# Loads of q and k move behind the threshold rows in SyncE's queue, with other ranks in the planner

## The chip, the core and the metric

The kernel runs on one core of one Trainium2 chip. The metric is device time in microseconds (us) of one execution; lower is better. Five instruction streams run side by side: TensorE (PE: matmuls), VectorE (DVE), ScalarE (ACT), GpSimd (POOL) and SyncE (SP, which here only issues DMA transfers). Each of them works through its own instructions strictly in the order in which they stand in the program, and waits at the head of its queue when data are missing.

## The reference

The input has 8 batches of 8 heads, 576 positions, 64 values per head, in float32. A thresholded attention feeds a feed-forward block:

```python
scores = scale * np.matmul(q, k.transpose(0, 1, 3, 2))
thresh = np.max(scores, axis=-1, keepdims=True) - tau
scores = np.where(scores >= thresh, scores, -1000000000.0)
scores = scores - np.max(scores, axis=-1, keepdims=True)
attn = np.exp(scores)
attn = attn / (np.sum(attn, axis=-1, keepdims=True) + 1e-09)
o = np.matmul(attn, v)                     # 64 heads
x = o.transpose(0, 2, 1, 3).reshape(4608, 512)
h = x @ w_in                               # 512 x 2048
g = h * (1.0 / (1.0 + np.exp(-1.702 * h)))
out = g @ w_out                            # 2048 x 512
```

The two weight matrices arrive in float64 (`wide` in the kernel): the kernel loads their bits and turns them into float32 itself.

## The kernel before

**Attention** works on 32 pairs of heads, numbered n from 0; four pairs make a batch, and "the fifth pair" is pair 4. One pair goes through these tasks (names of functions, lines of the profile):

- `load_qk(n, 0)` and `load_qk(n, 1)` (L246): q and k of the pair, four DMAs each, issued by SP (for pair 0, k by ACT). `load_v` (L256, L260): four DMAs on SP.
- `prep` (L358): DVE transposes q, then k, in blocks. This frees the raw buffer for the pair after next.
- `scores` (L382, tail L375): PE, four tiles of keys and a tail; `keep` (L405): ACT copies them to SBUF.
- `in_groups` (L419), `over_tiles`, `over_groups` (L425 to L438): DVE finds the maximum of each column. For pairs 0 to 7, `lower_rows` (L454, L459) subtracts tau and leaves a small tile `flat`; `row_out` (L471) sends it to DRAM as the threshold row, and `row_in` (L480, L482) fetches it back broadcast over all partitions, as `mb` and `mbt`. All three DMA steps are in SP's queue. From pair 8 on, `lower` and `spread_max` do this on DVE alone.
- `sub` (L489, L491): DVE subtracts the thresholds; `mask` (L500) and `exps` (L504): ACT.
- `values` and `sums_by_pe` (L518): PE multiplies by v, and for pairs 0 to 4 sums the weights; `one_row`, `spread_sums` (L547 to L568) and `place_x` (L585) on DVE put the normalized result into `xT`.

**The weights** come in 32 pieces of 128 x 512 values: 0 to 15 of `w_in`, 16 to 31 of `w_out`. `load_w` (L310, L311): POOL issues two DMAs of 512 KB for each into one of a few staging slots. `cv_ex` (L321), `cv_frac` (L335, L339) on DVE, `cv_power` (L329) on ACT and `cv_end` (L347) on DVE convert a piece, and `cv_end` frees its slot: pieces 6, 7, 8 and 9 wait for the slots of 0, 1, 2 and 3.

**The feed-forward block** starts when pairs 0 to 3 are placed: `first_blocks` does tokens 0 to 511 by plain matmuls, `mm1_0` (L640), `tanh` (L609), `gelu_0` (L646) and `mm2` (L622); `mm1_0(j)` needs the four converted pieces of its columns, and `mm2(i, p)` pieces 16+2p and 17+2p. After that, blocks of 256 tokens run with `mm1` (L600) and seven `product`s (L690) in Strassen's manner, while pairs 8 to 31 are threaded in between.

**The order on each engine** is not written out. A planner (`run_in_order`) plays the whole task graph through with fixed costs, and whenever an engine of this model is free it gives it the ready task of lowest rank. The rank is the pair's number plus an offset for the function's name (`EARLY` for pairs 0 to 7, `LATER` beyond, `CV` for conversions; weights have `W_IN`, `W_OUT`). The order of calls fixes the program's order. Costs, ranks and `after=` of a task act through this order alone: on the chip an instruction waits for the data and buffers that it uses and for those ahead of it on its engine.

```python
lq = task("SP", 2.0, r - 2.0, load_qk, n, 0, q0, take=own(n, "raw0"), lag=2.0)
lk = task("SP", 2.0 if n else 0.1, r - 2.0, load_qk, n, 1, q1, take=own(n, "raw1"), lag=2.0)
```

With `r = n`, loads of pair n rank two pairs ahead of its work, and start as soon as the raw buffers are free.

Of the kernel before, what the change touches and what calls it, by code (L numbers as in the profile page):

```python
# [30 lines left out]
def kernel(  # L31
# [37 lines left out]
    NPAIR = H // 2  # L69
# [59 lines left out]
    for x in ("raw0", "raw1", "qkT0", "qkT1", "mb"):  # L129
# [13 lines left out]
        "over_groups": -1.9,  # L143
        "sub": -0.29,
        "one_group": 0.95,
        "scores": -0.68,
        "spread_sums": 0.92,
        "sums_by_pe": 1.09,
        "in_groups": 0.61,
        "keep": -1.15,  # L150
    }
    LATER = {
        "in_groups": 0.38,
        "mask": -0.74,
    }
    CV = {
        "cv_power": 0.15,
    }

    def task(engine, cost, rank, f, *a, after=(), take=(), give=(), lag=0.06):  # L160
        if 0 <= rank < LAST:
            rank += CV.get(f.__name__, 0.0) + (EARLY if a[0] < 2 * NPAIR else LATER).get(f.__name__, 0.0)
        tasks.append((engine, cost, rank, f, a, [x for x in after if x is not None],
                      take, give, lag))
        return len(tasks) - 1
# [67 lines left out]
    def own(n, *pools):  # L233
        return tuple(x + "_apart" for x in pools) if n in APART else pools
# [527 lines left out]

    FFU = 1.722

    W_IN, W_OUT = (3.21, 1.53), (3.16, 2.2)
    ready_w, w_loads = [], []
    for i in range(len(pieces)):
        if i < n_in:
# [11 lines left out]
        m = task("ACT", 0.79, rank, cv_power, i, after=[e])  # L780
# [6 lines left out]
    tau_done = task("DVE", 1.0, -2.0, tau_terms, after=[warm])  # L787


    placed, ffn = {}, []  # L790
    last_mm2, t_ready = {}, []

    def first_blocks():
# [88 lines left out]
    for n in range(NP):  # L882
        gate = per_pair * (n - LEAD)
        after = ffn[gate : gate + 1] if gate >= 0 else []
        r = float(n)

        slow = 1.2 if n < NPAIR else 1.0
        q0, q1 = (nc.sync, nc.scalar) if n == 0 else (nc.sync, nc.sync)
        lq = task("SP", 2.0, r - 2.0, load_qk, n, 0, q0, take=own(n, "raw0"), lag=2.0)
        lk = task("SP", 2.0 if n else 0.1, r - 2.0, load_qk, n, 1, q1, take=own(n, "raw1"), lag=2.0)  # L890
        v_tail = f"v_t{n % 2}"
        lv = task("SP", 2.1, r - 1.2, load_v, n, take=("v_m", v_tail), lag=2.0)
        pq = task("DVE", 0.77, r, prep, n, 0, after=[lq], take=own(n, "qkT0"), give=own(n, "raw0"))
# [8 lines left out]
        for t in range(NKT + 1):  # L902
            tail = t == NKT
            copies = []
            if tail or n >= WHOLE:
# [5 lines left out]
                    take=("psA", "s_t") if tail else ("psA", "psA") + own(n, "s_m"),  # L911
                    give=own(n, "qkT0", "qkT1") + ("kd",) if tail else (),
                )
                after = [a]
                copies = [task("ACT", 0.65, r, keep, n, t, c, after=[a], give=("psA",)) for c in cs]
            else:
                for c in range(2):
# [3 lines left out]
                        take=("psA",) + (own(n, "s_m") if c == 0 else ()),  # L921
                    )
                    after = [a]
# [4 lines left out]
        if n < BY_DMA:  # L928
            a = task("DVE", 0.5, r, lower_rows, n, after=[a, tau_done], take=("row",))
            a = task("SP", 0.35, r, row_out, n, after=[a], lag=2.8)  # L930
            m = task(
                "SP", 1.5, r, row_in, n, after=[a], take=own(n, "mb") + ("mbt",), give=("row",),
                lag=5.0,
            )
        else:
            a = task("DVE", 0.7, r, lower, n, after=[a, tau_done])
            m = task("DVE", 1.38, r, spread_max, n, after=[a], take=own(n, "mb"))
        ws, subs = [], [m]
        for t in range(NKT + 1):
            tail = t == NKT  # L940
# [9 lines left out]
        if n < NPAIR:  # L950

            pv = den = None
            for t in every:
# [3 lines left out]
                    take=("psM", "psM") if first else (),  # L957
# [3 lines left out]
                    take=("psA",) if first else (), give=(back[t],) if t < NKT else ("s_t", "v_m", v_tail),  # L961
# [60 lines left out]
```

## Time and profile before

| | |
|---|---|
| six runs | median 1401.43 us, 1399.86 to 1404.77 |
| the profiled execution | 1402.07 us |
| its span in the profile | 1400.3 us (1.8 us lie around it) |
| PE busy | 1341.4 us, 96% of the span |
| DVE busy | 1037.6 us, 74% |
| ACT busy | 625.7 us, 45% |
| POOL busy | 281.9 us, 20% |
| granted TensorE clock, mean | 0.986 |

A row of the timeline tells start, length, engine, line, operation, tiles and count, and in brackets how long the engine was idle before it and what ended the wait. "SPq" and "POOLq" are the DMA-issuing queues. One fp32 matmul of the program appears as two records on PE.

### The profile page before, as it was taken

How to read it: one execution, taken by the hardware profiler on the slowest of the kernel's cores; microseconds unless marked ns; L12 is line 12 of the kernel's file. 1: busy time of each engine (PE TensorE's matmuls, PEld its weight loads, DVE VectorE, ACT ScalarE, POOL GpSimd, SP SyncE). 2: the span in 40 equal slices, each digit the busy share in tenths (PEclk: the TensorE clock that was granted, in tenths of full speed). 3: DMA queues.
4: the chain of work that ended last, by engine and by line, in shares of the span. 5: the costliest groups of instructions: out<-in, count | busy, mean ns of one | idle time of the engine just before them, and what ended most of it. 6: DMA issues, size and time to landing. Idle time of an engine off the chain costs nothing.

```text
span 1400.3 us, 18089 instructions
## 1 busy us (share of the span) xinstructions
PE 1341.4 (96%) x6856; PEld 1013.4 (72%) x6856; DVE 1037.6 (74%) x1773; ACT 625.7 (45%) x806; POOL 281.9 (20%) x374
## 2 busy tenths in 40 slices
PE   5648999999999999999999999999999999999998
PEld 3325774467777777777777777777777778888887
DVE  7859899898888888878988888888888886111111
ACT  5657454654444544455454455553545453100100
POOL 1201223123020122112120312020212212211211
PEclk9869999999999999999999999999999999999999
DMA  8656863311111111111111111101111100000000
GB/s 180 197 184 191 268 239 89 86 29 24 41 25 41 26 37 30 26 37 22 41 26 41 26 33 26 41 17 41 26 42 26 26 8 8 9 15 15 1 15 15
DMA packets 205727, 79.59 MB, mean 57 GB/s; under 512 B 192840, under 2 KB 192840, under 8 KB 205640
## 3 DMA queue, kind: packets, MB, share of 16 engines
q1 hardware_dynamic: 196072, 44.60, 14.9%
q0 software_dynamic: 7200, 33.55, 6.9%
q8 instruction: 54, 0.88, 0.2%
q10 hardware_dynamic: 2368, 0.30, 0.2%
q14 instruction: 33, 0.27, 0.1%
HBM read 68.93 MB, written 9.47 MB: 56 GB/s over the span
## 4 chain that ended last, share of the span: by engine, by line
PE 86%; DVE 7%; DMA 3%; issue 2%; SPq 1%; ACT 1%; POOL 0%; DVEq 0%; POOLq 0%; ACTq 0%
PE hps L600 32%; PE ops L690 28%; PE pv L518 10%; PE ps L382 9%; PE ops L622 3%; PE ps L375 2%; DVE s_m L489 1%; PE hps L640 1%; DVE part L419 1%; DVE arena L489 1%; SPq L246 1%; DMA w_out<-in_moe_w_in_dram 1%; DMA arena<-in_moe_w_out_dram 1%; DMA w_out<-in_moe_w_out_dram 1%; DVE qkT L358 0%
## 5 line engine op out<-in xcount | busy, mean ns | idle before, releaser
L600 PE MATMUL hps<-xT,w_in 128*128 128x256 f32 x2048 | 457.3, 381 | 0.0
L600 PEld LDWEIGHTS hps<-xT,w_in 128*128 128x128 f32 x2048 | 385.8, 190 | 67.3 <-issue 11.2
L419 DVE TRANSPOSE_TENSOR_REDUCE part<-s_m 128x36 f32<-128x1152 f32 x228 | 304.9, 1356 | 61.3 <-ACT s_m L405 57.9
L405 ACT COPY s_m<-ps 128x576 f32<-128x576 f32 x240 | 141.2, 642 | 243.3 <-PE ps L382 239.9
L690 PE MATMUL ops<-w_out,arena 128*128 128x256 f32 x1024 | 232.8, 381 | 0.0
L690 PEld LDWEIGHTS ops<-w_out,arena 128*128 128x128 f32 x1024 | 192.8, 190 | 33.6 <-issue 6.2
L609 ACT ACTIVATE th<-hps 128x512 f32<-128x512 f32 x144 | 85.4, 593 | 294.2 <-PE hps L600 280.7
L668 POOL TENSOR_TENSOR arena<-arena 128x256 f32<-128x256 f32 x64 | 58.6, 916 | 676.9 <-DVE arena L612 676.9
L500 ACT ACTIVATE s_m<-s_m 128x1152 f32<-128x1152 f32 x120 | 136.2, 1156 | 130.0 <-DVE s_m L489 129.2
L690 PE MATMUL ops<-arena 128*128 128x256 f32 x768 | 174.3, 381 | 0.0
L489 DVE TENSOR_TENSOR s_m<-s_m,mb 128x1152 f32<-128x1152 f32 x120 | 161.0, 1376 | 15.2 <-DMA mb<-row 14.5
L612 DVE SCALAR_TENSOR_TENSOR arena<-th,hps 128x512 f32<-128x512 f32 x128 | 87.2, 681 | 111.3 <-ACT th L609 109.3
L690 PEld LDWEIGHTS ops<-arena 128*128 128x128 f32 x768 | 144.8, 190 | 24.7 <-issue 4.6
L382 PE MATMUL ps<-qkT 64*128 64x288 f32 x960 | 150.1, 436 | 10.7 <-DVE qkT L358 9.4
L504 ACT ACTIVATE s_m<-s_m,shift,scl 128x1152 f32<-128x1152 f32 x120 | 157.3, 1342 | 0.9
L382 PEld LDWEIGHTS ps<-qkT 64*128 64x128 f32 x960 | 84.6, 191 | 69.0 <-issue 32.2
L518 PE MATMUL pv<-s_m,v_m 128*64 128x288 f32 x960 | 122.9, 409 | 0.0
L712 DVE SCALAR_TENSOR_TENSOR osb<-ops,osb 128x256 f32<-128x256 f32 x112 | 44.6, 410 | 99.5 <-PE ops L690 98.5
L518 PEld LDWEIGHTS pv<-s_m,v_m 128*64 128x64 f32 x960 | 66.5, 137 | 52.1 <-issue 8.8
L622 PE MATMUL ops<-w_out,arena 128*128 128x512 f32 x128 | 59.4, 613 | 2.8 <-DVE w_out L347 2.8
L640 PE MATMUL hps<-xT,w_in 128*128 128x256 f32 x256 | 58.0, 383 | 2.8 <-DVE arena L646 1.7
L670 POOL TENSOR_TENSOR arena<-arena 128x256 f32<-128x256 f32 x64 | 60.2, 941 | 0.0
(97 smaller groups left out, 1050.6 us busy)
## 6 DMA issues: line engine op xcount, KB each, us to landing
out_dram<-osb SPq DMA_DIRECT2D x36, 256.0 KB, 2.0
q_raw<-in_q_dram SPq DMA_DIRECT2D x120, 72.0 KB, 2.2
k_raw<-in_k_dram SPq DMA_DIRECT2D x116, 72.0 KB, 2.2
v_m<-in_v_dram SPq DMA_DIRECT2D x64, 128.0 KB, 2.3
w_out<-in_moe_w_in_dram POOLq DMA_DIRECT2D x12, 512.0 KB, 9.0
arena<-in_moe_w_out_dram POOLq DMA_DIRECT2D x12, 512.0 KB, 5.9
w_out<-in_moe_w_in_dram POOLq DMA_DIRECT2D x12, 511.6 KB, 9.9
arena<-in_moe_w_out_dram POOLq DMA_DIRECT2D x12, 511.6 KB, 7.0
```

Source lines behind the costliest of these rows:

```text
L382: nc.tensor.matmul(ps[:, h, 0:SH], lhsT=kT[ts(h, D), ts(t, P)], rhs=qT[ts(h, D), ts(c, SH)], start=True, stop=True,)
L405: nc.scalar.copy(out=o, in_=pss.pop((n, t, c))[:, :, 0:SH])
L419: nc.vector.tensor_reduce(out=o, in_=i, axis=AXL.X, op=op, apply_transpose=True)
L489: nc.vector.tensor_tensor(out=s, in0=s, in1=mb, op=ALU.subtract)
L500: nc.scalar.activation(out=s, in_=s, func=AF.Prelu, alpha=STEEP)
L504: nc.scalar.activation(out=s, in_=s, func=AF.Exp, scale=scl, bias=shift)
L518: nc.tensor.matmul(o[c][ts(h, D), 0:SH], lhsT=lhsT, rhs=rhs, start=(t == 0), stop=(t == NKT),)
L600: nc.tensor.matmul(hidden[j][:, ts(f, BLK)], lhsT=w_in[:, c, ds((f * HF + j) * P, P)], rhs=xTs[blk][:, c, :], start=(c == 0), stop=(c == N ...
L609: nc.scalar.activation(out=ths[j], in_=hidden[j], func=AF.Tanh, scale=GELU_SCALE / 2)
L612: nc.vector.scalar_tensor_tensor(out=g[:, :, j, :], in0=two(ths.pop(j)), scalar=1.0, in1=two(hidden.pop(j)), op0=ALU.add, op1=ALU.mult,)
L622: nc.tensor.matmul(acc[i], lhsT=g0[:, j, ts(i, P)], rhs=w_out[:, j, :], start=(j == 0), stop=(j == NFC - 1),)
L690: nc.tensor.matmul(banks[k][:, ts(o, HM)], lhsT=left[:, j, :], rhs=right[:, j, :], start=(j == 0), stop=(j == HF - 1),)
```

## The change

Three things are edited. Loads of q and k from pair 4 on get a dependency: they come after `spread[n - 2]`, which is `row_in` for pairs up to 7 and `spread_max` beyond. The planner's cost of such a load goes from 2.0 to 3.5 for pairs 4 to 7. And eight offsets and the rank of the first weight load are changed or added.

```diff
-        "scores": -0.68,
-        "spread_sums": 0.92,
-        "sums_by_pe": 1.09,
-        "in_groups": 0.61,
+        "scores": -1.85,
+        "spread_sums": 0.09,
+        "sums_by_pe": 1.93,
+        "in_groups": 1.37,
         "keep": -1.15,
+        "over_tiles": 0.88,
     }
     LATER = {
         "in_groups": 0.38,
         "mask": -0.74,
+        "prep": 0.98,
     }
     CV = {
         "cv_power": 0.15,
+        "cv_end": -0.38,
     }
...
-    W_IN, W_OUT = (3.21, 1.53), (3.16, 2.2)
+    W_IN, W_OUT = (3.92, 1.53), (3.16, 2.2)
...
+        behind = [spread[n - 2]] if n >= NPAIR else []
+        cost = 3.5 if NPAIR <= n < 2 * NPAIR else 2.0
+        lq = task("SP", cost, r - 2.0, load_qk, n, 0, q0, after=behind, take=own(n, "raw0"), lag=2.0)
+        lk = task(
+            "SP", cost if n else 0.1, r - 2.0, load_qk, n, 1, q1, after=behind,
+            take=own(n, "raw1"), lag=2.0,
+        )
...
+        spread[n] = m
```

No instruction is added or taken away; every engine gets the same instructions in another order. SP's queue from the first threshold row on (q4 is `load_qk(4, 0)`, row 2 is `row_out(2)` and `row_in(2)`, v2 is `load_v(2)`):

```
before: row 0, q4 k4, row 1, v2, q5 k5, row 2, v3, row 3, v4, q6 k6, v5, row 4, q7 k7, v6, row 5
after:  row 0, row 1, v2, row 2, q4 k4, v3, row 3, q5 k5, v4, v5, row 4, q6 k6, v6, row 5, q7 k7
```

DVE's queue, with "cv" for the conversion of a piece, "max" for `in_groups` and "fold" for `over_tiles`, `over_groups` and `lower_rows`, which end with the row's `flat` tile:

```
before: ... fold 1, prep 3, max 2, sub 1 (0-2), one_row 0, sub 1 (3-4), place 0 among cv 0 to 2 without
        their ends, prep 4, max 2 tail, fold 2, ends of cv 0 to 2, one_row 1, cv 3, most of cv 4,
        sub 2, place 1, end of cv 4, max 3, fold 3, ex and frac of cv 5 to 8 (ex 9), end of cv 5,
        sub 3 with one_row 2 in it, place 2, prep 5, cv 9 to 14 with one_row 3 in them,
        max 4 (0-1), place 3, ...
after:  ... prep 3, max 1 tail, fold 1, max 2, cv 0, cv 1, sub 1 with place 0 in it, max 2 tail, fold 2,
        cv 2 and 3, max 3 (0) among them, most of cv 4, sub 2 with one_row 1 in it, place 1, prep 4,
        end of cv 4, max 3 (1-4), fold 3, cv 5 to 7, ex 8, sub 3 with place 2 in it, prep 5,
        rest of 8, cv 9 to 13, ex 14, one_row 3, place 3, rest of 14, cv 15, max 4, ...
```

On PE, `sums_by_pe` and `values` of pairs 0 to 3 stand tile by tile in turn, where before all sums of a pair came first; the first blocks follow behind pair 3 as before. POOL's order is nearly unchanged: the copies `prep_kd` of pairs 4, 5 and 6 stand at other places among the weight loads.

More of the change, by code (lines that the diff above doesn't have):

```diff
@@ L787 @@
     tau_done = task("DVE", 1.0, -2.0, tau_terms, after=[warm])
-    placed, ffn = {}, []
+    placed, spread, ffn = {}, {}, []
     last_mm2, t_ready = {}, []
@@ L888 @@
         q0, q1 = (nc.sync, nc.scalar) if n == 0 else (nc.sync, nc.sync)
-        lq = task("SP", 2.0, r - 2.0, load_qk, n, 0, q0, take=own(n, "raw0"), lag=2.0)
-        lk = task("SP", 2.0 if n else 0.1, r - 2.0, load_qk, n, 1, q1, take=own(n, "raw1"), lag=2.0)
+        behind = [spread[n - 2]] if n >= NPAIR else []
[5 more added lines that the diff above has]
+        )
         v_tail = f"v_t{n % 2}"
```

## Prediction

> **What bounds the kernel now.** First the page's slices: where is PE not full?
>
> ```profile
> PE   5648999999999999999999999999999999999998
> ...
> DVE  7859899898888888878988888888888886111111
> ...
> PEclk9869999999999999999999999999999999999999
> DMA  8656863311111111111111111101111100000000
> ```
>
> A slice is 35 us. Only the first four show idle PE; there DVE is the fuller engine and DMA is busy. In windows, PE is busy for 175.9 us up to 230 us (54 us idle), and for all but about 5 us of the rest. So a gain can come only from the start, and a loss can come anywhere. Next, SP's timeline in that stretch, to see what the rows wait for:
>
> ```profile
> 26.68 14.13 SPq L246 DMA_DIRECT2D k_raw<-in_k_dram  x4
> 40.90 0.37 SPq L471 DMA_DIRECT2D row<-flat  x1
> ...
> 60.04 4.01 SPq L246 DMA_DIRECT2D q_raw<-in_q_dram  x4
> 64.17 14.36 SPq L246 DMA_DIRECT2D k_raw<-in_k_dram  x4
> 78.63 0.59 SPq L471 DMA_DIRECT2D row<-flat  x1
> 81.36 0.36 SPq L480 DMA_DIRECT2D mb<-row  x1
> ...
> 146.65 9.74 SPq L246 DMA_DIRECT2D q_raw<-in_q_dram  x4
> 156.43 10.25 SPq L246 DMA_DIRECT2D k_raw<-in_k_dram  x4
> ```
>
> Then DVE's timeline: when is a row ready, when is it back, when are the four pairs placed?
>
> ```profile
> 46.38 3.90 DVE L489 TENSOR_TENSOR arena<-arena 128x1152 f32<-128x1152 f32 x3 [4.08 <-DMA arena<-row]
> ...
> 63.17 0.23 DVE L459 STREAM_TRANSPOSE flat<-flat 32x64 f32<-32x64 f32 x1
> ...
> 85.38 5.16 DVE L489 TENSOR_TENSOR s_m<-s_m,mb 128x1152 f32<-128x1152 f32 x4 [14.50 <-DMA mb<-row]
> ...
> 100.25 0.23 DVE L459 STREAM_TRANSPOSE flat<-flat 32x64 f32<-32x64 f32 x1
> ...
> 136.26 0.91 DVE L585 TENSOR_TENSOR xT<-pv,rc 128x256 f32<-128x256 f32 x4
> ```
>
> Row 2 is ready at 63.4 and leaves at 78.63, behind q5 and k5, which SP needs 18.5 us to issue while weights stream (POOL issued pieces 3 to 9 from 53.8 to 70.8). DVE stands for 14.50 us. Row 1, ready at 35.9, leaves at 40.90 behind k4: 4.08 us. Last PE's timeline:
>
> ```profile
> 136.70 19.91 PE L640 MATMUL hps<-xT,w_in 128*128 128x256 f32 x90 [1.06 <-DVE xT L585]
> ...
> 225.93 4.34 PE L622 MATMUL ops<-w_out,arena 128*128 128x512 f32 x6 [2.82 <-DVE w_out L347]
> ```
>
> The first blocks go on when pair 3 is placed, and stop once, for the last weight piece.
>
> **Up to row 3: less waiting, same work.** Read off start to start, DVE's steps are: a transpose 0.66 us, a max 1.26 (tail 0.66), a fold 2.2, a `sub` 1.26 (tail 0.67), a conversion 0.34 + 1.06 + 0.61, `one_row` 0.96, `spread_sums` 1.0, `place_x` 0.86. Both orders have exactly the same tasks ahead of row 3's `flat`: 72.2 us by these steps. Before, it is done at 100.4; the waits are 5.96 (tau), 3.06 and 0.36 (first copies), 4.08 and 14.50. The first three, 9.4, stay.
>
> Row 1 now leaves at once: 30.3 us of work stand ahead, so at 39.7. Until its `sub`, DVE has 6.5 us (two maxima, cv 0 and 1); a row took 5.5 (40.90 to 46.38). Wait 0. Uncovered, it would cost 5.5.
>
> Row 2: 48.3 us of work, so ready at 57.7. DVE has 6.7 us (cv 2, 3, most of 4, one max); a row takes 5.5, or 6.75 beside weights (78.63 to 85.38), and under 8.0 in the slowest stretch (201.81 to the `sub` at 209.76). Wait 0 to 1.3; I take 0.1, from the same row.
>
> The four loads that moved are not free, because their `prep` stands in DVE's queue. Behind it are the end of cv 4, the maxima and fold of pair 3, and for PE `scores` of pair 4. q4 and k4 start behind row 2, at 57.7 + 2.7 (row out) + 1.8 (row in) = 62.2. `prep` 4 is wanted at 73.1 (63.6 of work + 9.5). In a quiet stretch the issue takes 4.2 (q2 and k2) and landing 2.4: wait 0. At the longest pair of loads, 20.0 (146.65 to 166.68): 84.6, wait 11.5. Nearest is k4 before: it ended 12.3 us after the last of three pieces (28.5 to 40.8). Here two pieces are in flight, 8 and 9, whose slots come free at the ends of cv 2 and 3, so two thirds of that from 64.5: 72.7, landed 75.1. I take 2.0. For `cv_end` 0 to 2, each of which waits for ACT's `cv_power`, I add 0.4. Row 3 is ready at 72.2 + 9.4 + 0.1 + 2.0 + 0.4 = 84.1 instead of 100.4: 16.3 us earlier.
>
> **To pair 3 placed.** DVE's work here is 31.1 us, not 35.4: two maxima of pair 4 and the end of cv 14 now come later. Row 3 is covered by 6.5 us (most of cv 5 to 8). q5 and k5 start at 84.1 + 4.5 = 88.6; `prep` 5 is wanted at 99.0. Quiet: wait 0. Longest: 111.0, wait 12. Nearest are the two issues with three to five pieces beside them, 16.3 (24.48 to 40.81) and 13.8 (120.06 to 133.90): 15, landed 106.0. I take 6.5, since q can be transposed before k lands. With the 1.3 that this stretch lost before beyond its work, placed at 84.1 + 31.1 + 6.5 + 1.3 = 123.0 instead of 137.2: 14.2 earlier. The loads of q6, k6 and q7, k7 have over 20 us until `prep` 6 and some 10, with the weights gone, until `prep` 7: cost 0, at most 2.
>
> On the sharing there is a rule: the Trainium skill, "DMA: Bandwidth & Descriptors", section "Queues, rings and completion order", says that each DMA engine goes round robin between the queues' rings, packet by packet. It speaks against this change, as small packets of q and k get no faster by standing behind a row. By it I would give q5 and k5 the 18.5 us of before, wait 10.5, and the time would be 4.0 us longer.
>
> **PE from there.** Before, PE had done 6 passes (1.4 us) when it went on at 136.70; the same point is now 122.6 + 1.4 = 124.0. Until it stopped at 223.1 it worked 84.7 us and idled 1.7. The same set of matmuls lies ahead of that point in the new order: 210.4. The last `cv_end` was 80.6 us after that of piece 15 (145.25 to 225.87); DVE's work between them is 68.8 us, 67.9 before. Piece 15 now ends at 126.7, so the last at 208.2, before PE asks. Instead of 225.93 PE is there at 210.4: **15.5 us saved**. If the conversions came 5 us later, 12.7 would remain.
>
> The gap also cost clock: 32 passes from 102.15 took 5.79 us, with 0.83 granted in that window, and 4.10 at 181.58. I count nothing, because DVE sets the pace there. The Trainium skill, "TensorE: Matmul & The Clock Gate", Part 1, gives a cold PE half its clock for about 3.4 us of work, an estimated 1.7 us per gap; by it the time would be 1.7 lower.
>
> **The rest of the run.** PE is full, so moved ranks can only lose. Critical is `prep` of k: from pair 9 on it stands behind the read of product 5 (or `gelu` 4), while PE still has `values` of the pair before (5.0 us) ahead of `scores`: 5.0 - 0.4 - 0.66 leaves 4.0, and 3.3 to 4.1 over all pairs. Before, the same count gives 1.3 to 3.8, with one wait of 1.1 us in the whole trace. Cost 0. Stores and v loads are passed by no more than one load of q or k and wait for buffers anyway: 0. The changed rank of the first weight load moves nothing ahead of piece 10.
>
> Sum: 1402.07 - 15.5 = 1386.6 for an execution like the profiled one, which was 0.6 above the median: **1386.0**.
>
> **Rivals.**
>
> - *The loads come in time* (17%). Waits of 2.0 and 6.5 vanish, as for loads issued in quiet stretches. Saving 24, time 1377.4. For it: pieces now start earlier, by the copy `prep_kd` 3, and may be gone. Against it: every pair of loads beside weights took 14 to 20 us.
> - *The stall moves to `prep`* (14%). Both pairs of loads take the longest row, 20.0: waits of 11.5 and 12 instead of 8.5 together. The saving falls to about 0.5, and the time is near 1401. For it: 18.5 and 20.0 were the two latest pairs. Against it: fewer pieces in flight.
> - *The steady part starts to wait* (10%, slower). k's transpose comes late once per pair, PE waits at `scores` of pairs 9 to 31 for 1.1 us, the one such wait of the trace: 23 x 1.1 = 25, time 1411. It decides from 0.7 us per pair on. For it: DVE is over 19 of 20 us busy in many windows. Against it: margins grew.
> - *It does not do what it says* (4%). Row 2 comes back no earlier, since its own transfers queue behind the weights on the DMA engines: 14.5 return, 1400.
>
> The forecast keeps 55%. The range takes in the first rival's 1377.4 with a little below, and ends at 1399, short of the two dearer mechanisms. Below 0.2% (2.8 us) a measurement can't tell a change: faster by more 84%, within 5%, slower 11%.
>
> **What would show it.** Right: row 2 leaves within 1 us of its `flat`, near 58 us; DVE's wait for `mb` shrinks from 14.5 to about 0; row 3's `flat` is done near 84, pair 3 is placed near 123, `mm2` reaches its last piece near 210; new waits of DVE on q or k of 2 and 6.5 us. Wrong: such waits over 10 us each, placing after 135, or PE waits for `qkT` after 300 us.

## The result, and the profile after

The changed kernel takes 1397.12 us (median of 22 runs, 1394.62 to 1399.52), the kernel before 1401.44 us (46 runs): a ratio of 0.9969, 95% interval 0.9962 to 0.9976. It is faster by 4.3 us, 0.3%, where 15.5 us were forecast. The profiled execution took 1398.51 us, with a span of 1396.7 us.

The slices, as before (35 us each):

```profile
PE   5868999899999999999999999999999999999998
...
DVE  7888999998888888888888888888888887111111
...
PEclk9888999999999999999999999999999999999999
DMA  6875863202111111111112011111111100000000
```

PE is fuller in the second and third slice, and has an 8 in the eighth slice (245 to 280 us), where it had 9 before. SP's timeline (start, length, queue, line, operation):

```profile
61.88 0.30 SPq L474 DMA_DIRECT2D row<-flat  x1
66.97 0.36 SPq L483 DMA_DIRECT2D mb<-row  x1
...
68.66 6.45 SPq L249 DMA_DIRECT2D q_raw<-in_q_dram  x4
...
97.35 12.92 SPq L249 DMA_DIRECT2D k_raw<-in_k_dram  x4
```

Lines of the changed kernel stand three higher. Row 2 leaves the moment its `flat` is done, 17 us earlier than before, and q4, k4 follow it. But the way out alone takes 5.1 us (61.88 to 66.97), where it took 2.7 before. DVE's timeline shows what that does:

```profile
75.08 5.16 DVE L492 TENSOR_TENSOR s_m<-s_m,mb 128x1152 f32<-128x1152 f32 x4 [6.36 <-DMA mb<-row]
...
92.05 0.23 DVE L462 STREAM_TRANSPOSE flat<-flat 32x64 f32<-32x64 f32 x1
...
129.25 0.95 DVE L588 TENSOR_TENSOR xT<-pv,rc 128x256 f32<-128x256 f32 x4
```

The wait for `mb` fell from 14.50 to 6.36 us, not to 0. PE's timeline behind the point where it had stopped before:

```profile
204.92 20.76 PE L625 MATMUL ops<-w_out,arena 128*128 128x512 f32 x48
...
280.21 2.29 PE L385 MATMUL ps<-qkT 64*128 64x288 f32 x8 [5.41 <-DVE xT L588]
282.44 6.05 PE L521 MATMUL pv<-s_m,v_m 128*64 128x288 f32 x32
...
295.15 23.14 PE L603 MATMUL hps<-xT,w_in 128*128 128x256 f32 x104
```

The stop of 2.82 us for the last weight piece is gone (48 records of `mm2` run through), but a new one of 5.41 us stands at 280 us: the scores of pair 8 wait for a PSUM buffer that is free only when pair 6 is placed. Behind it PE is slow: 6.05 us for the 32 passes that take 4.10 elsewhere, with a granted clock of 0.50 from 280 to 285 us.

The last line is the best milestone: `mm1` of block 2 starts at 295.15 us. In the kernel before it stands here:

```profile
298.07 15.70 PE L600 MATMUL hps<-xT,w_in 128*128 128x256 f32 x72
```

From there to the end of the span it is 1101.6 us, before 1102.2. All that the change does, it does ahead of that point. In the same places (us, profiled executions; the forecast's block 2 and end are the values of before less 15.5):

| | before | forecast | after | after, tensor sums moved (e6) | and row 2 by DVE (e12) |
|---|---|---|---|---|---|
| `sub` of pair 2 starts | 85.38 | 64.5 | 75.08 | 72.53 | 66.49 |
| row 3 ready | 100.48 | 84.1 | 92.28 | 91.58 | 87.03 |
| pair 3 placed | 137.2 | 123.0 | 130.2 | 128.3 | 125.1 |
| last piece converted | 225.9 | 208.2 | 213.8 | 207.8 | 204.1 |
| block 2 starts | 298.07 | 282.6 | 295.15 | 282.74 | 279.02 |
| span ends | 1400.3 | 1384.8 | 1396.7 | 1384.3 | 1380.3 |

### The profile page after: what moved, and what is told of

It reads as the page before. It is cut to its first block, busy times and chain, and to the rows that moved or that the text cites. A ratio compares the mean times of both kernels' runs of the same rounds, so it can differ in the third digit from the quotient of the medians.

```text
span 1396.7 us, 18070 instructions
## 1 busy us (share of the span) xinstructions
PE 1347.5 (96%) x6856; PEld 1017.0 (73%) x6856; DVE 1054.6 (76%) x1773; ACT 631.7 (45%) x806; POOL 307.0 (22%) x374
## 4 chain that ended last, share of the span: by engine, by line
PE 81%; DVE 12%; DMA 3%; SPq 1%; issue 1%; ACT 0%; ACTq 0%; DVEq 0%
PE hps L603 31%; PE ops L693 28%; PE pv L521 9%; PE ps L385 8%; DVE part L422 3%; PE hps L643 2%; DVE s_m L492 2%; PE ps L378 2%; SPq L249 1%; DMA row<-flat 1%; DMA mb<-row 1%; DMA k_raw<-in_k_dram 1%; DVE fold L440 1%; PE den L521 0%; DVE qkT L361 0%
## 5 line engine op out<-in xcount | busy, mean ns | idle before, releaser
L603 PE MATMUL hps<-xT,w_in 128*128 128x256 f32 x2048 | 457.7, 381 | 0.1
L693 PEld LDWEIGHTS ops<-w_out,arena 128*128 128x128 f32 x1024 | 192.3, 190 | 36.1 <-issue 10.4
L492 DVE TENSOR_TENSOR s_m<-s_m,mb 128x1152 f32<-128x1152 f32 x120 | 184.1, 1570 | 8.4 <-DMA mb<-row 7.7
L671 POOL TENSOR_TENSOR arena<-arena 128x256 f32<-128x256 f32 x64 | 52.6, 822 | 618.1 <-DVE arena L615 618.1
L693 PE MATMUL ops<-arena 128*128 128x256 f32 x768 | 171.0, 379 | 0.0
L693 PEld LDWEIGHTS ops<-arena 128*128 128x128 f32 x768 | 145.9, 190 | 19.8
L521 PE MATMUL pv<-s_m,v_m 128*64 128x288 f32 x960 | 127.2, 416 | 0.0
L678 POOL TENSOR_TENSOR arena<-arena 128x512 f32<-128x512 f32 x32 | 62.4, 1954 | 111.4 <-PE ops L693 111.1
L366 POOL COPY kd<-qkT 64x64 f32<-64x64 f32 x60 | 25.3, 421 | 222.7 <-DVE qkT L361 193.3
L673 POOL TENSOR_TENSOR arena<-arena 128x256 f32<-128x256 f32 x64 | 60.2, 940 | 0.0
```

The source lines that it names most:

```text
L492: nc.vector.tensor_tensor(out=s, in0=s, in1=mb, op=ALU.subtract)
L521: nc.tensor.matmul(o[c][ts(h, D), 0:SH], lhsT=lhsT, rhs=rhs, start=(t == 0), stop=(t == NKT),)
L603: nc.tensor.matmul(hidden[j][:, ts(f, BLK)], lhsT=w_in[:, c, ds((f * HF + j) * P, P)], rhs=xTs[blk][:, c, :], start=(c == 0), stop=(c == N ...
L678: nc.gpsimd.tensor_tensor(out=u, in0=a12, in1=u, op=ALU.subtract)
L693: nc.tensor.matmul(banks[k][:, ts(o, HM)], lhsT=left[:, j, :], rhs=right[:, j, :], start=(j == 0), stop=(j == HF - 1),)
```

## The experiments

Three orders are in play: the dependency of the loads, the ranks, and where POOL does `t_sum`. These are eight additions of weight tiles (`t_sum(x, k)`, x from 0 to 3, two halves each, 2.3 us a half), which the products of block 2 need. All times below are medians of 4 to 12 timed runs. The ratios compare each with runs of the kernel before made beside it; by them a difference between two experiments can come out up to some 2.5 us off from that of the two medians. Where tasks are moved by hand, the planner's order is written down and the named tasks are moved in it; all other engines keep the changed kernel's order.

**e1, the ranks alone.**

```diff
-        behind = [spread[n - 2]] if n >= NPAIR else []
-        cost = 3.5 if NPAIR <= n < 2 * NPAIR else 2.0
+        behind = []
+        cost = 2.0
```

> The changed kernel with one part undone: loads of q and k no longer come after the row of the pair two ahead, and the planner's cost for them is 2.0 again; the new ranks stay. Theory A (the place in SP's queue carries the gain): rows 1 or 2 stand behind loads again, DVE waits 10 us or more for mb in one of them, and the time is back at 1400 to 1404. Rival B (the ranks carry it): within 0.2% of the changed kernel, 1395 to 1399.

Measured: 1408.52 us, 1.0051 of before (1.0039 to 1.0064). The ranks alone make it slower by 7.4 us. DVE still waits 18.0 us for `mb`, and PE now waits twice for a placed pair, 4.84 us at 245 and 4.54 us at 286 us.

**e2, the dependency alone.** All offsets and `W_IN` as before; dependency and cost as changed.

> The kernel before with the dependency and the load cost alone, ranks as before. Theory A: row 2 leaves SP within 1 us of its flat, the DVE wait for it falls from 14.5 to 3 to 8 us, and the time is 1394 to 1399, as with the whole change. Rival B: without the ranks the planner's order leaves new waits elsewhere and the time stays at 1400 to 1406.

Measured: 1390.03 us, 0.9925 (0.9911 to 0.9939). The dependency alone brings 11.1 us, and 11.1 less 7.4 is 3.7, about the whole change's 4.3. So the ranks take most of the gain back. Row 2 leaves at 58.91 and `sub` 2 starts at 72.44: 13.5 us, as slow as with the ranks.

**e3, where the sums stand.** The wait for pair 6 has a cause that the two timelines show side by side. POOL in the changed kernel:

```profile
261.55 5.98 POOL L366 COPY kd<-qkT 64x64 f32<-64x64 f32 x2 [35.44 <-DVE qkT L361]
267.61 4.68 POOL L666 TENSOR_TENSOR arena<-w_out,arena 128x1024 f32<-128x1024 f32 x2
```

and DVE, which folds the sums of pair 6 at the same moment:

```profile
267.48 2.53 DVE L433 TENSOR_TENSOR red<-red,part_t 64x18 f32<-64x18 f32 x2
270.04 2.29 DVE L440 COPY fold<-red 64x36 f32<-64x36 f32 x1
272.37 2.29 DVE L441 TENSOR_TENSOR red<-red,fold 64x36 f32<-64x36 f32 x1
274.69 2.25 DVE L440 COPY fold<-red 32x36 f32<-32x36 f32 x1
```

Steps that take 0.2 to 0.4 us elsewhere take 2.3 each: the length of one half of a `t_sum`. These steps last 9.7 us where 1.2 would do, and pair 6 is placed that much later. The `prep_kd` copy ahead of it, normally 0.53 us, lasted 5.98 beside four `sub`s, and so the sums began just with the fold. e3 puts `t_sum` 2 and 3 behind the next such copy:

```diff
+        if n == 9:
+            tasks[t_ready[4]][5].append(pd)
```

> The changed kernel with the second half of POOL's sums of w_out (t_sum 2 and 3) behind the copy prep_kd of pair 9 instead of pair 8 in POOL's queue; no other engine's order changes. Theory P (in the changed kernel four tiny DVE folds of pair 6 lasted 2.3 us each beside these sums, 267.5 to 277.0, and PE then waited 5.41 us for place_x 6): the folds last 0.2 to 0.4 us, place_x 6 ends near 271 instead of 280, PE's wait of 5.41 is gone and the time is 1388 to 1392. Rival O (DVE simply has too much work ahead of place_x 6, and the folds only fill what is waited for anyway): PE still waits 3 us or more there, the time is 1395 to 1399. If the sums now collide with pair 9's work, a part of the gain is lost there.

Measured: 1398.42 us, 0.9978 (0.9967 to 0.9990): nothing gained. The fold of pair 6 was short again and block 2 started at 283.67 us, but the sums then fell on the fold of pair 8 (three steps of 2.23, 2.29 and 4.90 us). PE's timeline:

```profile
321.48 2.29 PE L385 MATMUL ps<-qkT 64*128 64x288 f32 x8 [6.58 <-DVE xT L588]
```

The mechanism was right and the remedy wrong: the collision moved with the sums.

**e4, the weights beside row 2.** A one-column read of pair 2's `mb` on POOL holds pieces 5 to 7 until that row is back.

```diff
+        tasks.append(("POOL", 0.1, 0.0, see_row, (2,), [], (), (), 0.1))
+        order.insert(find(order, "row_in", 2) + 1, len(tasks) - 1)
+        for i in (5, 6, 7):
+            behind = ("see_row", 2) if i == 5 else ("load_w", i - 1)
+            move(order, ("load_w", i), behind)
```

> The changed kernel with weight pieces 5, 6 and 7 held on POOL until row 2 has come back (a copy of one column of its mb by POOL stands ahead of them); every other order is the same. Theory R (the row's own two transfers are slowed by the weight packets beside them: 13.2 us from flat to mb in the changed kernel, 5.5 in a quiet stretch): 5.5 to 7.5 us from flat to mb, DVE's wait for mb falls from 6.36 to 0 to 1, and fold 3 ends near 86 instead of 92.3; the time falls by 2 to 6 us unless the later weights eat it at cv 5 to 7. Rival S (the row is slow by itself in this stretch, at its DRAM round trip or in SP's queue): still over 10 us from flat to mb, fold 3 near 92.

Measured: 1400.05 us, 0.9992 (0.9982 to 1.0002). DVE's timeline:

```profile
66.41 5.16 DVE L514 TENSOR_TENSOR s_m<-s_m,mb 128x1152 f32<-128x1152 f32 x4
...
86.65 0.78 DVE L383 STREAM_TRANSPOSE qkT<-k_raw 128x576 f32<-128x576 f32 x1 [10.82 <-DMA k_raw<-in_k_dram]
```

Row 2 was out in 1.2 us instead of 5.1, `sub` 2 started 6.8 us after the row had left instead of 13.2, and the wait of 6.36 us is gone (the first line has no bracket). So the weights in flight are what slows the row. The held pieces then stood beside k4, and its `prep` waited 10.8 us, where it had waited for nothing: row 3 was ready at 94.5, 2.3 us later than in the changed kernel.

**e5, the sums at a safe place.** POOL holds `t_sum` 2 until pair 6 is placed and `t_sum` 3 until pair 7 is placed, so that they lie beside maxima.

```diff
+        for n, x in ((6, 2), (7, 3)):
+            tasks.append(("POOL", 0.1, 0.0, see_place, (n,), [], (), (), 0.1))
+            order.insert(find(order, "place_x", n) + 1, len(tasks) - 1)
+            move(order, ("t_sum", x, 0), ("see_place", n))
+            move(order, ("t_sum", x, 1), ("t_sum", x, 0))
...
+    def see_place(n):
+        x = (n // NPAIR * S + S - 1) // BLK
+        nc.gpsimd.tensor_copy(out=seen, in_=xTs[x][:, n % NPAIR, (n // NPAIR + 1) * S % BLK - 1 :][:, 0:1])
```

> The changed kernel with one edit on GpSimd alone: the sums t_sum 2 are held until pair 6 is placed and t_sum 3 until pair 7 is placed (a one-column read of the placed tile holds them), so that they lie beside VectorE's maxima and not beside its folds. Theory S (the four seconds lost by 295 us are lost where these sums hold VectorE's short copies): the fold of pair 6 falls from 9.4 us to about 2, pair 6 is placed near 270 instead of 279, TensorE's wait of 5.41 us at the scores of pair 8 goes, with some 3 us of cold clock behind it, and nothing takes its place: 1389 us (1387 to 1391.5). Theory R (the order of VectorE's work under the new ranks costs by itself, wherever the sums lie): the wait comes back at pair 8 as it did with the sums put off behind its k, 1395 to 1399 us.

Measured: 1389.32 us, 0.9902 (0.9886 to 0.9918), 7.8 us less than the changed kernel, with two instructions more and the order of every other engine as it was. POOL's timeline, and after it DVE's:

```profile
271.58 4.69 POOL L689 TENSOR_TENSOR arena<-w_out,arena 128x1024 f32<-128x1024 f32 x2 [0.22 <-issue]
```

```profile
270.10 0.95 DVE L606 TENSOR_TENSOR xT<-pv,rc 128x192 f32<-128x192 f32 x4
```

Pair 6 is placed at 270.1 instead of 279.1, PE's wait of 5.41 is gone and nothing takes its place. Block 2 starts at 286.13.

**e6, the first sums too.** As e5, and `t_sum` 0 and 1 behind the copies of pair 7's k.

```diff
+        move(order, ("t_sum", 0, 0), ("prep_kd", 7))
+        for a, b in (((0, 0), (0, 1)), ((0, 1), (1, 0)), ((1, 0), (1, 1))):
+            move(order, ("t_sum",) + b, ("t_sum",) + a)
```

> As the kernel before this one in the list, and t_sum 0 and 1 behind the copies of pair 7's k as well, so that they no longer lie beside the last weight conversion (2.58 and 2.72 us for two steps of 0.41 and 0.69) and the subtractions of pair 5 (8.47 us for 5.1). VectorE is some 7 us earlier at 224 us. Theory S: TensorE waited only 1.0 us for that, so the time is that of the kernel before this one less 0 to 2 us: 1386 to 1390. Theory R: 1395 to 1399 us.

Measured: 1386.33 us, 0.9882 (0.9868 to 0.9896). The four `sub`s of pair 5 take 5.12 us instead of 8.47, the last piece is converted at 207.8 instead of 213.8, and behind 163 us PE waits nowhere until block 2. In the profiled executions e6 reaches block 2 12.4 us before the changed kernel; 1.9 of these were there when pair 3 was placed, up to where both have the same order, so the sums account for about 10.5.

**e7, which ranks.** The change touches seven offsets (not eight, as counted above) and the rank of the first weight load. Here the five in `EARLY` are as before; `prep` in `LATER`, `cv_end` and `W_IN` stay changed.

> The changed kernel with the ranks of the first eight pairs as they were; the later prep's rank, cv_end's and the first weight load's stay changed. If the cost of the ranks that the two halves alone showed (7.4 us) comes from the ranks of the first eight pairs: as the dependency alone, 1390 us (1388.5 to 1392). If it comes from the prep of the later pairs or from cv_end: 1395 to 1399 us. If both share it: 1392 to 1395.

Measured: 1401.65 us, 1.0002 (0.9990 to 1.0015). A miss on all sides: the three remaining edits cost 11.6 us against e2, so the ranks cannot be split in this way. One part can be read: here `t_sum` 0 begins at 220.99 and holds the fold of pair 5 for 4.5 us, the last piece's conversion stands behind that fold, and PE waits 5.56 us for it. The rest of the 11.6 was not followed up.

**e8, a better version of the dependency alone.** As e2, with pair 7's k transposed one place earlier, since its PE wait of 3.64 us stood behind a fold that `t_sum` 1 held for 3.15 us.

```diff
+        move(order, ("prep", 7, 1), ("prep", 7, 0))
```

> The kernel before with the dependency alone (1390.0 us), and on VectorE the transpose of pair 7's k one place earlier than the sum's fold of pair 5, which t_sum holds for 3.15 us. If TensorE's wait of 3.64 us for that transpose cost what it shows: 1386 us (1384.5 to 1387.5). If the time is given back at the next wait, the placing of pair 5 or 6: 1389 to 1391 us.

Measured: 1388.77 us, 0.9899 (0.9885 to 0.9913). By the medians that is 1.3 of the hoped 4 us; by the two ratios it is some 3.6, and the runs of the two kernels overlap, so how much came is open. A wait of 2.80 us for the placing of pair 5, behind the same fold, which is still held, took over from the wait for k.

**e9, the ranks alone with the sums moved.** e1 with the moves of e6.

> The changed kernel without the dependency (the new ranks alone, 1408.5 us with the sums where the planner puts them), and the sums t_sum 0 to 3 moved on GpSimd as in the kernel that ran 1386.3. Theory S: the new ranks cost only by where they let the sums fall; TensorE's two waits for a placed pair, 4.84 and 4.54 us, and the cold clock behind them go: 1398 us (1396 to 1401), no slower than the kernel before. Theory R (the order costs by itself when the rows come back late): 1404 to 1409.

Measured: 1393.41 us, 0.9935 (0.9922 to 0.9948), 15.1 us less than e1, more than expected. Both waits for a placed pair are gone, though DVE still waits 19.8 us for `mb`. So the ranks do not cost by themselves: with the sums out of the way the kernel with the new ranks alone is some 9 us faster than the kernel before. How much of this is the ranks' own is not told apart, since the sums cost the kernel before something too (see below).

**e10, the control.** The kernel before with the moves of e6.

> The kernel before with the sums held in the same way (t_sum 0 and 1 behind pair 7's k, 2 and 3 until pairs 6 and 7 are placed). It is the control: in the kernel before the last two sums lie beside maxima already and TensorE waits for no placed pair behind 137 us, so moving them should bring nothing by itself: 1399 to 1403. If the sums held the kernel before as well, 1394 to 1398, and the gain of 10.8 us from moving them would not be the change's own loss.

Measured: 1404.87 us, 1.0015 (1.0005 to 1.0025). No gain. The moved `t_sum` 0 and 1 fall on a fold there, and PE waits 3.77 us for pair 5. The safe place depends on DVE's order. As a control it is not clean: it shows that these places are not safe in the order of before, and not what well-placed sums would bring there.

**e11, the dependency alone with the first sums moved.** e8, with `t_sum` 0 and 1 behind the copies of pair 7's k.

> The dependency with the old ranks and pair 7's k one place earlier (1388.8 us), and t_sum 0 and 1 moved behind the copy of that k. The fold of pair 5 was held 2.51 us and TensorE waited 2.80 us for pair 5: theory S gives 1386 us (1384.5 to 1387.5), about the time of the new ranks with the sums moved, so that the ranks are worth nothing either way once the sums lie well. If the last weight conversion or the next placing takes the wait over: 1388 to 1390.

Measured: 1395.79 us, 0.9951 (0.9937 to 0.9965), 7.0 us slower than e8. With the old ranks, the fold of pair 5 follows directly on that k. So the move put the sums on the fold that they should have left. POOL, DVE and PE:

```profile
217.81 4.68 POOL L680 TENSOR_TENSOR arena<-w_out 128x1024 f32<-128x1024 f32 x2
```

```profile
217.99 2.23 DVE L455 TENSOR_TENSOR red<-red,fold 64x36 f32<-64x36 f32 x1
220.26 2.27 DVE L454 COPY fold<-red 32x36 f32<-32x36 f32 x1
```

```profile
229.97 2.29 PE L399 MATMUL ps<-qkT 64*128 64x288 f32 x8 [7.52 <-DVE xT L602]
```

A mistake of mine, and the cleanest trial of the cause: the same work in the same order on every other engine, one collision more, a PE wait of 7.5 instead of 2.8 us, and 7 us of the whole.

**e12, row 2 without memory.** e6, with pair 2's thresholds spread by `lower` and `spread_max` on DVE.

```diff
+        if n == 2:
+            lower(n)
+            spread_max(n)
+            return
```

(in `lower_rows`; `row_out` and `row_in` return for pair 2)

> The changed kernel with the sums moved (1386.3 us), and pair 2's thresholds spread by VectorE itself, as the kernel does from the ninth pair on, not through memory. It measures the term that the prediction mis-sized: the row's way out and back beside weights, 13 us where 6.75 were taken, with 6.79 us of waiting. VectorE gets some 2.3 us more work (a lower, a spread of 1.38, a split tail) and q and k of pair 4 can leave at 51 us instead of 65.7. If that row sets the pace up to 130 us: fold 3 some 4 to 5 us earlier, 1381 to 1383 us. If TensorE or the loads of pair 4 or 5 take the wait over: 1385 to 1388.

Measured: 1381.99 us, 0.9856 (0.9834 to 0.9878), 4.3 us less than e6 and the best of all. DVE's timeline:

```profile
66.49 5.16 DVE L521 TENSOR_TENSOR s_m<-s_m,mb 128x1152 f32<-128x1152 f32 x4
...
86.80 0.23 DVE L487 STREAM_TRANSPOSE flat<-flat 32x64 f32<-32x64 f32 x1
```

The first line has no bracket: no wait. Row 3 is ready 4.5 us earlier than in e6, and 4.3 us arrive at the end. The edit also lets q4 and k4 leave at 50 us, so the row and the loads are not told apart here.

## Why the prediction was right and wrong

**Right:** that a gain can come only up to some 230 us; that the row leaves with its `flat` (row 1 at 39.71, forecast 39.7); that PE no longer stops for the last piece; that the steady part loses nothing (1101.6 us for 1102.2 from block 2 on); the sign. The time lies inside the range too, but by luck: the range ended at 1399 to leave out two other mechanisms, and the one that took the gain back is not in it.

**Wrong: "the rest of the run", cost 0.** This is the step that failed. The prediction looked in the moved ranks for late transposes of k from pair 9 on, and there were none. The cost lay earlier and elsewhere: between the point where PE had stopped (record 30 of `mm2`, at 225.93 before and 214.4 after) and block 2, the changed kernel needs 80.8 us for 72.1. Of these 8.6 us, 6.8 are three waits for a placed pair (5.41, 1.00, 0.37), 3.0 the slow passes behind the longest, and 0.5 the 32 passes for pair 5 at 225.61 (4.56 us for 4.10), less 1.7 for the slow clock behind the old stop. With the 4.0 us by which PE reached that point late (see the rows' way, below), and 0.6 won from block 2 on, this makes up the 12 us that the profiled execution misses of the 15.5. The prediction called POOL's order nearly unchanged and left it there. It should have asked what DVE now does while POOL adds. Moving eight POOL additions brought 10.8 us (e6: 1386.33, close to the forecast's 1386.0, though partly by luck, see the clock below).

The evidence stood in the profile of before, unread. DVE's conversion of the last piece there:

```profile
218.65 2.59 DVE L335 TENSOR_SCALAR arena<-arena 128x512 int32<-128x512 int32 x1
221.28 2.73 DVE L339 SCALAR_TENSOR_TENSOR arena<-arena 128x512 int32<-128x512 int32 x1
```

and POOL beside it:

```profile
218.53 4.93 POOL L663 TENSOR_TENSOR arena<-w_out 128x1024 f32<-128x1024 f32 x2 [7.32 <-DVE w_out L347]
```

Two steps of 0.42 and 0.69 us took 2.59 and 2.73, so 4.2 of the time up to the last `cv_end`, for which PE then stopped 2.82 us, came from this collision and not from late weights. e10 shows it: with these sums moved, the last piece of the kernel before is converted at 222.5 instead of 225.9, and PE runs past the old stop (but stops later, for pair 5):

```profile
210.30 15.61 PE L648 MATMUL ops<-w_out,arena 128*128 128x512 f32 x36
```

**Wrong: the rows' way beside weights.** Terms of the sum that were mis-sized: row 2 took 13.2 us from `flat` to `sub` (6.75 taken; 13.5 in e2, 13.6 in e6, 8.6 in e5), a wait of 6.4 for 0.1, and row 1 10.4 us (5.5 taken), a wait of 3.05 for 0. Row 1's delay begins with one more collision of POOL and DVE. The copy `prep_kd` 2 stands ahead of pieces 0 to 2 in POOL's queue; here it is in the changed kernel and in e6, which have the same order up to this point:

```profile
30.33 5.46 POOL L366 COPY kd<-qkT 64x64 f32<-64x64 f32 x2 [10.90 <-PE ps L378]
```

```profile
29.83 0.52 POOL L387 COPY kd<-qkT 64x64 f32<-64x64 f32 x2 [9.51 <-PE ps L399]
```

Beside `sub` 0 (29.62 to 34.7) it took 5.46 us and held the pieces up; in e6 it came 0.7 us ahead of `sub` 0. The later the pieces left, the longer row 1's way out: 1.3 to 1.4 us where the copy took 0.52 (e3, e6, e12, no wait for row 1), 3.8 to 4.1 where it took 2.11 (e1, e4, e9), 5.3 to 5.6 where it took 5.46. A shift of 1.4 us between the two engines decides it. Against this, q and k came sooner than feared: 3.8 us of waiting instead of 8.5. Row 3 was ready at 92.28 instead of 84.1 and pair 3 placed at 130.2 instead of 123.0; at PE's old stop the lag was still 4.0 us (214.4 for 210.4). e4 shows the cause, weights in flight; e12 puts the price of row 2's way, together with the earlier loads, at about 4.3 us.

**Wrong in the other direction: the clock behind a gap.** The prediction weighed this for the gap ahead of 102 us (the 0.83 quoted there is of 100 to 110 us; over the 5.79 us it was 0.71) and counted nothing, there or elsewhere. But the old stop had cost clock as well: the six records behind it took 4.34 us, at a granted clock of 0.64, against 2.6 at the 0.43 us each of the 48 records in the changed kernel. That is 1.7 us, which the change saved. The rule weighed there, in the Trainium skill's "TensorE: Matmul & The Clock Gate", Part 1, had given an estimated 1.7 us per gap. Here it was the better guide than my reason against it. It is also why e6 could meet the forecast: e6 reached the old stop 2.3 us late (212.7 for 210.4) and won 2.1 us from there to block 2, so that two misses nearly cancel.

**The rivals.** The loads did come in better time, though not wholly. The stall did not move to `prep` in the changed kernel (3.8 us), only in e4, where it took 10.8 us. The rival of a steady part that waits did not come about. The last rival (row 2 held by weights on its own way) was half right: 6.4 of the 14.5 us returned.

## What to carry to other kernels

When an order moves, look at pairs of engines and not only at each engine: a reordering that leaves an engine's own list unchanged can still slide its long instructions beside another engine's short, urgent ones. Read the mean of an operation by its stretched members; a step of 0.2 us that takes 2.3 somewhere names its neighbour. And judge two parts of a change apart: here the ranks alone ran 7 us slower than the kernel before, and 9 us faster than it once eight additions stood elsewhere.

## What the runs showed of the hardware

Short DVE operations with two inputs, copies and scalar operations took up to the length of one POOL addition, 2.2 to 2.7 us, where they stood beside one. Reductions (1.3 us) and transposes (0.7 to 0.8) beside the same additions did not stretch: the first transpose in e2's stretch, beside `t_sum` 1, took 0.73. The other way round, a pair of POOL copies of 0.53 us took 5.98 beside four `sub`s in a row, and 5.46 or 2.11 beside `sub` 0 (2.11 in e1, e4 and e9). The Trainium skill's "SBUF — State Buffer", section "Who interferes with whom", states that the two engines share a port pair which one instruction holds to its end while the other engine is blocked, for DVE operations with two inputs and for copies and scalar operations in a two-port mode, but not for `tensor_reduce`; these runs agree, with 2.3 us a time (no run shows in which mode the copies ran). What I had not expected is the leverage: 8.5 us of DVE lost at one fold (9.7 us for 1.2, undone in e5) and some 6 us at another (e11 against e8) were 7.8 and 7.0 us of the whole kernel, since a placed pair frees the buffer that PE wants next, and PE then restarts slowly (a granted clock of 0.50 from 280 to 285 us).
